# Attention and token/channel mixer on one core: two pools for the attention's tiles, three weight pairs decoded ahead, low parts on VectorE, tile addresses at multiples of 64 bytes

## The chip, the core and the metric

The kernel runs on one core of a Trainium2 chip. The metric is the time of one execution on the device in microseconds (us), lower is better. The core has a matmul engine (TensorE, PE in the profile), VectorE (DVE), ScalarE (ACT), GpSimd (POOL) and SyncE (SP), which issues all DMAs of this kernel. PEld is the loading of a matmul's weights, which the profile lists beside PE.

## What is computed

Causal attention with a decay, then a two-layer mixer over tokens and one over channels. The inputs are float32, and `B, H, S, D = 8, 8, 576, 64`; the model width is 512, the token mixer's inner width 256, the channel mixer's 1536.

```python
scores = (q @ k.T) / sqrt(D) + cum[:, None] - cum[None, :]   # cum = cumsum(log(clip(f)))
scores = where(causal, -1e9, scores)
attn = softmax(scores)
x = concat_heads(attn @ v)                         # (B, S, 512)
h = maximum(x.T @ w_tok1, 0) @ w_tok2              # over tokens
u = x + h.T
out = u + maximum(u @ w_ch1, 0) @ w_ch2            # over channels
```

The mixer's four weight matrices arrive as 64-bit floats in two 32-bit words each.

## The kernel before, in words

**Precision.** A float32 value is split into a high part that a fast matmul takes (fp32r) and a low part, the value minus the high part. A product is three matmuls: high x high, low x high, high x low. So nearly every tile comes in a pair: `hl`, `t1h`/`t1l`, `w1r[:, 0]`/`w1r[:, 1]`, and so on. ScalarE or GpSimd writes the high parts (`hi_act` L288, `hi_pool` L291); GpSimd's `lo_pool` (L294, `tensor_tensor` subtract) or VectorE's `lo_dve` (L297) and `lo_relu` (L300) write the low ones. The first four heads (`FQ`, `FV`) use plain fp32 matmuls and skip the split.

**Attention.** The 64 heads (`HB`) go one after the other, a pair of heads to a load. For each head: q and k are loaded and split, gathered by DMA (`k<-hl`, L533) into `k1` and `k2`; scores in five row blocks (L560), the causal mask and row minimum on VectorE (L567), the exponential on ScalarE (L574), the normalisation on GpSimd (L602), the transposes of the probabilities on PE (L616), their high and low parts, and the product with v (L684 to 698), folded into `xt`.

**Mixer.** After four heads of a batch follows half of its token mixer (`mixer`, L887: transposes L913, `tok1` L946, `tok2` L970), and after eight its other half and the first `F1 = 2` of the 12 blocks of the channel mixer (`ch1` L1015, `ch2` L1043); `u` and the partial sums are stored to DRAM. The other `F2 = 10` blocks run over all 4608 tokens at the end, in nine chunks of 512 columns (`up` L815 with matmuls L832 to 834, `down` L842 with L853 to 855). There each of the ten steps of a chunk takes 24 matmuls of 512 columns, 12 of `up` and 12 of `down`.

**Decoding weights.** Every block of the weights is turned from 64-bit words to fp32 and split by `decode` (L359): a load into `d_raw` (three buffers); s1 on ScalarE (L377); s2, s3, s4 on VectorE (L381, L385, L389); s5 (L393) on GpSimd for the 15 early blocks and on VectorE for the 20 late ones; s6 on VectorE (L397); the high part on ScalarE, the low part on GpSimd (L295). `d_g` (two buffers) holds the work between s1 and the low part. The 20 late decodes make the pairs `w1r[i]`, `w2r[i]` for i = 0 to 9, which the last stage needs in this order.

**Memory.** SBUF is full during the attention. The attention's tiles (`ATT`, L884) lie in one pool, `att`. When its last reader is done, `swap` (L1178) gives the whole pool back and lays `w1r`, `w2r` and `hid` there. In the plan this is an operation `gate` that follows every operation on an attention tile (L763 to 768), and the loads of the late decodes wait for it (`rd=["gate"] if late`, L368). Pools lay tiles in steps of 32 bytes: `ident` begins at byte 16,512 (258 x 64), and behind the small tiles `nmin`, `sums`, `rec` and `lower` (32 bytes) `t1h` begins at byte 19,872 (310 x 64 + 32). All tiles behind it have sizes that are multiples of 64 bytes, and so all of them begin at odd multiples of 32.

**What sets the order.** Nothing is scheduled on the chip. A planner (`Plan`, L82) simulates the five engines with costs for each operation (`mm_`, `tp_`, `d_act`, `d_dve`, `d_ptt`, L263 to 278) and starts, on each engine, the ready operation with the lowest priority number whose buffers are free. Priorities are the head's number plus an offset for the kind of operation (`OFF`, L23), plus one for the kind and the head in its batch (`STEP`, L29; `MIX`, L56, for the mixer). The simulated order is emitted as it is, each engine runs its own list in this order, and semaphores make it wait where data are not ready.

**Fills.** `fill` (L344) puts matmuls of `ident` with itself, of no use to the result, at the lowest priority: 60 of them, each two passes of 64 columns, not before 3.5 us of the plan and with 110 ns added after each.

Of the kernel before, what the change touches and what calls it, by code (L numbers as in the profile page):

```python
# [9 lines left out]
F32 = mybir.dt.float32  # L10
# [8 lines left out]
    FILL=60, EP=3, DB=0, DLAST=1, K0=0, F1=2, FQ=4, FV=4, LAG=4.11, n_raw=1, n_vr=2, n_hl=1, n_k1=2, n_k2=2, n_vv=2,  # L19
    E_hi='POOL', E_lo='POOL', E_vh='ACT', E_vl='POOL', E_nrm='POOL', n_pr=3, n_p34=2, n_p2=2, n_p1=1, n_p0=1, n_low=1,  # L20
    n_ring=12, n_part=4, n_xt=2, n_d_raw=3, n_d_g=2, n_hid=3, DEC3=7.97, SPREAD=10.82, SPREADA=5.72,
)
OFF = dict(  # L23
    load=-14.74, kh=45.74, kl=85.6, qh=-115.26, ql=-16.97, vh=-125.16, vl=123.08, s4=4.74, s3=5.74, s2=-18.62, mn=13.82,
    ex=6.93, rec=-24.46, nrm=-192.34, t3=3.49, t2=-86.91, t1=-83.66, t0=-30.56, hl=-22.74, av=6.05, fold=-23.02,
    fpe=3.13, lo0=-62.2, fev=-150.17, u=-45.03, dec=67.5, dec2=50.29, cd=-13.03, vload=-5.0,
# [3 lines left out]
    cd=(-18.28, 30.34, 0.0, -1.59, -7.08, 20.8, -4.45, -19.73),  # L30
    kh=(-13.25, -1.98, -14.84, -31.71, -0.08, 0.16, -4.73, -16.57),
    kl=(0.37, 23.35, 3.6, 16.35, -22.44, 19.22, -9.3, 14.29),
    s4=(-0.24, 11.93, 15.18, 0.0, 0.23, -18.99, 59.85, 19.27),
    s3=(-8.42, -2.23, -16.47, 3.1, -5.05, 3.69, -8.16, -5.03),
    s2=(-8.9, 5.94, 2.9, 7.66, -73.57, -5.62, -37.16, -17.06),
    mn=(-2.85, -2.59, -1.3, 27.24, -15.18, -23.44, 55.89, -2.52),
    ex=(8.73, 7.79, -3.58, -4.16, -24.69, 9.71, 15.25, -0.82),
    rec=(22.8, -0.87, 7.74, -8.31, -3.51, 14.08, 0.0, -15.0),
    nrm=(-0.65, -0.14, -0.26, -56.35, 0.93, 8.15, 15.62, 16.52),
    t3=(-0.21, -6.67, 3.6, -5.38, 7.93, -4.68, -63.6, 0.91),  # L40
    t2=(-8.37, 4.56, -28.86, -0.92, -2.2, 21.66, 9.34, -1.7),
    t1=(2.24, -60.09, 14.99, -0.13, 1.6, -10.19, -0.26, 18.37),
    t0=(-17.86, -45.26, -1.03, 6.15, -93.62, -1.53, 2.02, -1.16),
    hl=(-14.65, 3.9, 19.52, -2.31, 1.89, 47.46, 1.51, 21.22),
    av=(63.33, -8.47, -19.49, -11.27, -9.11, -24.95, -27.57, -16.6),
    fold=(0.0, -4.01, 0.0, 15.75, -6.44, -20.04, 54.83, -5.7),
    load=(0.44, -22.57, -32.0, 0.63, -21.63, 0.0, 24.57, -17.55),
    vload=(-3.66, -1.79, -4.01, 2.15, 1.75, -12.36, 4.68, -26.36),
    qh=(10.91, -1.93, 0.0, 6.38, 17.8, 15.93, -0.05, 13.38),
    lo0=(-19.38, -0.5, -4.34, -1.11, -3.76, 0.0, -12.38, 21.57),  # L50
    ql=(9.89, -8.85, -13.87, 15.7, 1.76, 0.12, 0.0, 25.12),
    vh=(-0.25, 1.03, -17.17, 0.0, -0.24, -3.2, 8.2, 72.18),
    vl=(6.57, -2.23, 2.05, 5.49, -2.18, -5.19, -2.35, -1.08),
# [3 lines left out]
    (-22.1, -17.41, -3.1, 2.93, 26.12, -0.37, 12.64, 5.86),  # L57
    (-10.33, 23.64, -53.62, -1.9, -30.51, 42.72, 7.26, -41.94, 25.22, -8.12, -7.09, 12.01, 3.03, 3.93, -39.21, -12.17, 8.18, 11.69, 19.72, 142.59, -29.87, -72.3, 9.6, -13.06, 8.97, 78.59, -11.05, 125.89),
# [19 lines left out]
class Op:  # L78
    __slots__ = ("eng", "dur", "head", "tail", "lat", "fn", "prio", "bufs", "need", "outs", "ready", "start", "idx")


class Plan:  # L82
# [43 lines left out]
    def run(self, slots):  # L126
# [18 lines left out]
        tail = dma_at = 0.0  # L145
# [30 lines left out]
        while left:  # L176
            moved = False
            for e, lst in ready.items():
# [23 lines left out]
                engine_at[e] = end  # L202
                heapq.heappush(events, (end, heap_id, None))
# [44 lines left out]
def build(nc, env, dims):  # L248
# [35 lines left out]
    def dma(prio, fn, nbytes, **k):  # L284
        return p.op("SP", k.pop("dur", 475), prio, fn, lat=nbytes / k.pop("rate", 360), **k)
# [24 lines left out]
    def decay():  # L310
# [12 lines left out]
        p.op("ACT", d_act(S, False), pr, lambda: nc.scalar.activation(row(0), row(0), AF.Ln), wr=["f"], bufs=[w])  # L323
        p.op(
# [3 lines left out]
        p.op("DVE", d_dve(S, True), pr, lambda: nc.vector.tensor_scalar(at(cc)[:, 0, :], c(), 1.0, None, op0=ALU.mult), rd=["c"], wr=["ch"], bufs=[cc])  # L328
        p.op("DVE", d_dve(S), pr, lambda: lo_dve(at(cc)[:, 1, :], c(), at(cc)[:, 0, :]), rd=["c", "ch"], wr=["cl"], bufs=[cc])
# [14 lines left out]
    def fill(i):  # L344
        av = Buf("av")
        p.op(
            "PE", [tp_(64, 64)] * 2, 1e6 + i, lambda: nc.tensor.matmul(at(av)[:64, :64], E["ident"][:, :64], E["ident"][:, :64], start=True, stop=True),
            rd=[("fill", i - 1)], wr=[("fill", i)], bufs=[av], lat=110, at=3500.0,
        )
# [9 lines left out]
    def decode(prio, loads, w, hi, lo, tok, late=False):  # L359
# [7 lines left out]
        for i, (rows, cols, src) in enumerate(loads):  # L367
            dma(prio - 1.0, lambda a=(rows, cols, src): ld(*a), nb / len(loads), rd=["gate"] if late else [], wr=[(rb, i)], bufs=[rb])  # L368
# [856 lines left out]
```

## Time and profile before

| | |
|---|---|
| median of three runs | 1129.55 us (1127.94 to 1131.58) |
| the profiled execution | 1131.37 us |
| its span, first to last instruction | 1129.6 us |
| TensorE clock granted, mean over the span | 0.979 |
| busy: PE, VectorE, ScalarE, GpSimd | 96%, 56%, 49%, 49% of the span |

A row of a group reads: line, engine, operation, output <- inputs with shapes, x count | busy us, mean ns of one | idle time of the engine just before these instructions, and what ended it. A row of a stage gives start:end, length, then for each engine its busy time with the number of instructions, the granted TensorE clock (1.00 is full), the share of time in which the DMA engines were busy, and GB/s. A wait reads: who <- whom, us in total, how often, the longest. In the timeline and in the chain of work that ended last, a row begins with its start and its length in us. Busy time of PE is modelled, since matmuls overlap: their pace is read from their starts or from a stretch without gaps.

### The profile page before, as it was taken

How to read it: one execution, taken by the hardware profiler on the slowest of the kernel's cores; microseconds unless marked ns; L12 is line 12 of the kernel's file. 1: busy time of each engine (PE TensorE's matmuls, PEld its weight loads, DVE VectorE, ACT ScalarE, POOL GpSimd, SP SyncE). 2: the span in 40 equal slices, each digit the busy share in tenths (PEclk: the TensorE clock that was granted, in tenths of full speed). 3: DMA queues.
4: the chain of work that ended last, by engine and by line, in shares of the span. 5: the costliest groups of instructions: out<-in, count | busy, mean ns of one | idle time of the engine just before them, and what ended most of it. 6: DMA issues, size and time to landing. Idle time of an engine off the chain costs nothing.

```text
span 1129.6 us, 18680 instructions
## 1 busy us (share of the span) xinstructions
PE 1084.4 (96%) x6422; PEld 940.4 (83%) x6422; DVE 637.1 (56%) x1598; ACT 554.8 (49%) x1440; POOL 552.4 (49%) x633
## 2 busy tenths in 40 slices
PE   8988899999999999999997889999999999999998
PEld 5667789999999998999996668888888888888886
DVE  5888887888778787787869993121212121211111
ACT  4677787888787887878854342111111111111110
POOL 4667797877787785977725335130303021211010
PEclk7998899999999999999998999999999999999999
DMA  8487767777777677777635444130303030302011
GB/s 203 111 197 166 191 148 205 204 170 193 207 190 211 173 197 182 189 202 191 156 120 177 139 133 140 46 112 1 113 1 112 1 112 1 112 2 73 20 56 38
DMA packets 70223, 146.65 MB, mean 130 GB/s; under 512 B 10048, under 2 KB 27456, under 8 KB 69104
## 3 DMA queue, kind: packets, MB, share of 16 engines
q1 hardware_dynamic: 70128, 145.45, 47.7%
q8 instruction: 51, 0.84, 0.3%
q14 instruction: 44, 0.36, 0.1%
HBM read 63.46 MB, written 28.31 MB: 81 GB/s over the span
## 4 chain that ended last, share of the span: by engine, by line
PE 66%; DVE 10%; DMA 9%; POOL 7%; issue 3%; ACT 2%; SPq 2%; DVEq 0%; POOLq 0%; ACTq 0%
DMA k<-hl 8%; PE pair L855 7%; PE bank L833 7%; PE pair L853 7%; PE pair L854 7%; PE bank L834 7%; PE bank L832 6%; PE bank L616 5%; PE bank L560 4%; DVE d_g L389 2%; PE pair L560 2%; POOL hl L489 2%; POOL pr L602 2%; PE pair L698 2%; PE pair L696 2%
## 5 line engine op out<-in xcount | busy, mean ns | idle before, releaser
L301 DVE SCALAR_TENSOR_TENSOR hid<-bank,hid 128x512 fp32r<-128x512 f32 x90 | 62.1, 690 | 331.9 <-ACT hid L289 331.9
L295 POOL TENSOR_TENSOR ring<-xt,ring 128x512 fp32r<-128x512 f32 (+1 forms) x68 | 92.6, 1378 | 273.2 <-ACT ring L289 272.7
L289 ACT ACTIVATE hid<-bank 128x512 fp32r<-128x512 f32 x90 | 53.7, 596 | 336.4 <-PE bank L834 336.4
L602 POOL TENSOR_SCALAR pr<-pr,rec 128x576 f32<-128x576 f32 (+4 forms) x320 | 167.4, 543 | 38.9 <-DVE rec L595 17.1
L832 PE MATMUL bank<-ring,w1r 128*128 128x512 f32 x360 | 141.2, 392 | 7.0 <-DVE hid L301 6.9
L289 ACT ACTIVATE p<-bank 128x384 fp32r<-128x384 f32 (+1 forms) x300 | 127.0, 474 | 30.1 <-PE bank L616 21.8
L616 PE MATMUL bank<-ident,pr 128*128 128x128 f32 (+1 forms) x960 | 137.7, 276 | 3.7 <-ACT pr L574 1.5
L833 PE MATMUL bank<-ring,w1r 128*128 128x512 f32 x360 | 140.8, 391 | 0.3 <-POOL w1r L295 0.3
L855 PE MATMUL pair<-hid,w2r 128*128 128x512 f32 x360 | 140.3, 390 | 0.7 <-DVE hid L301 0.7
L834 PE MATMUL bank<-ring,w1r 128*128 128x512 f32 x360 | 140.8, 391 | 0.0
L853 PE MATMUL pair<-hid,w2r 128*128 128x512 f32 x360 | 140.3, 390 | 0.0
L854 PE MATMUL pair<-hid,w2r 128*128 128x512 f32 x360 | 140.1, 389 | 0.0
L298 DVE TENSOR_TENSOR p<-bank,p 128x384 fp32r<-128x384 f32 x180 | 105.7, 594 | 39.1 <-ACT p L289 38.9
L574 ACT ACTIVATE pr<-bank,nmin 128x320 f32<-128x320 f32 (+3 forms) x256 | 117.9, 469 | 15.9 <-DVE nmin L567 10.3
L616 PEld LDWEIGHTS bank<-ident,pr 128*128 128x128 f32 (+1 forms) x960 | 107.7, 132 | 17.4 <-issue 4.3
L567 DVE CUSTOM_DVE_ANT_0 bank<-bank,mask 128x192 f32<-128x192 f32 (+3 forms) x256 | 106.5, 432 | 22.4 <-PE bank L560 20.8
L560 PE MATMUL bank<-k 128*128 128x320 f32 x480 | 86.2, 302 | 11.1 <-DMA k<-hl 8.4
L560 PEld LDWEIGHTS bank<-k 128*128 128x128 f32 x480 | 71.5, 178 | 22.6 <-issue 9.4
L832 PEld LDWEIGHTS bank<-ring,w1r 128*128 128x128 f32 x360 | 67.9, 189 | 23.4 <-DVE hid L301 9.6
L855 PEld LDWEIGHTS pair<-hid,w2r 128*128 128x128 f32 x360 | 67.5, 188 | 15.4 <-DVE hid L301 1.5
L833 PEld LDWEIGHTS bank<-ring,w1r 128*128 128x128 f32 x360 | 67.8, 188 | 14.6 <-POOL w1r L295 0.8
L834 PEld LDWEIGHTS bank<-ring,w1r 128*128 128x128 f32 x360 | 67.9, 189 | 14.3
(124 smaller groups left out, 2498.1 us busy)
## 6 DMA issues: line engine op xcount, KB each, us to landing
k<-hl SPq DMA_DIRECT2D x180, 288.0 KB
raw<-in_qk SPq DMA_DIRECT2D x30, 576.0 KB
vr<-in_v SPq DMA_DIRECT2D x32, 320.0 KB
ud<-xt SPq DMA_DIRECT2D x8, 1152.0 KB
pd<-part SPq DMA_DIRECT2D x32, 288.0 KB
out_t<-part SPq DMA_DIRECT2D x36, 256.0 KB
d_raw<-in_w_ch SPq DMA_DIRECT2D x12, 512.0 KB
d_raw<-in_w_ch SPq DMA_DIRECT2D x40, 128.0 KB
```

The costliest lines, as they stand in the source:

```text
L289: nc.scalar.activation(out, in_, func, scale=scale)
L560: nc.tensor.matmul(ps[:m, of : of + w], k[:, 0, i0 : i0 + m], k[:, 1, j0 : j0 + w], start=(x == 0), stop=(fq or x == 1))
L567: nc.vector.tensor_tensor_reduce(x, x, E["mask"][:m, a : a + w], -1.0 / D**0.5, 3e38, op0=ALU.add, op1=ALU.min, accum_out=E["nmin"][sm][:m ...
L574: nc.scalar.activation(at(pr)[:m, poff[t] : poff[t] + w], at(buf)[:m, of : of + w], AF.Exp, bias=E["nmin"][sm][:m, t : t + 1], scale=-1.0, ...
L602: nc.gpsimd.tensor_scalar(x, x, r, 0.0, op0=ALU.mult, op1=ALU.add)
L616: nc.tensor.transpose(out, at(pr)[:, poff[i] + start[j] : poff[i] + end[j]], E["ident"])
L832: nc.tensor.matmul(q, wh[:, c, :], h_, start=(c == 0), stop=False)
L833: nc.tensor.matmul(q, wl[:, c, :], h_, start=False, stop=False)
L834: nc.tensor.matmul(q, wh[:, c, :], l_, start=False, stop=(c == NC - 1))
L853: nc.tensor.matmul(q, wh, h_, start=(i == i0), stop=False)
L854: nc.tensor.matmul(q, wl, h_, start=False, stop=False)
L855: nc.tensor.matmul(q, wh, l_, start=False, stop=(i == NF - 1))
```

## The change

- The attention's tiles go into two pools. `raw`, `hl`, `k1`, `k2` and `cc`, which only the scores need, lie in one at the right end of SBUF, the others in one at the left. Each has its own gate. The first, after the last operation on a score tile, frees room for `w1r`, `w2r` of the first three pairs (`PAIRS0 = 3`) and `hid`; the second for the other seven.
- A late decode's load and steps s1 to s6 wait for no gate; the high part, the first that writes into the new pool, waits for its own.
- The low part of a late decode is `lo_dve` on VectorE, before `lo_pool` on GpSimd.
- The planner knows a port that GpSimd and the marked VectorE operations share: none of them starts in the plan while another holds it. It assumes slower DMAs (300 bytes per ns after 360, 220 after 200 for gathers), and the lag between scores and transposes is 3.3 heads after 4.11. All offsets are new, and the first and the last batch and each decode have offsets of their own.
- 120 fills, not before 8.5 us of the plan, without the added 110 ns.
- One exponential into `warm` after the logarithm of `f`. `warm` also takes 32 bytes behind `lower`, so that the tiles behind it begin at multiples of 64 bytes; `even0` and `even1` (32 bytes each) do the same for the pools at the right end.
- The two row blocks that share a bank are scored as 0, 3 and no longer as 3, 0.

```diff
-    FILL=60, EP=3, DB=0, DLAST=1, K0=0, F1=2, FQ=4, FV=4, LAG=4.11, ...
+    FILL=120, EP=3, DB=0, DLAST=1, F1=2, FQ=4, FV=4, LAG=3.3, ...
...
-    def op(self, eng, dur, prio, fn, rd=(), wr=(), bufs=(), lat=0, at=0.0):
+    def op(self, eng, dur, prio, fn, rd=(), wr=(), bufs=(), lat=0, at=0.0, port=False):
         o = Op()
+        o.port = port or eng == "POOL"
...
-                    if o.ready > t or (best is not None and (o.prio, o.idx) >= (best.prio, best.idx)):
+                    if o.ready > t or (o.port and port_at > t) or (best is not None and (o.prio, o.idx) >= (best.prio, best.idx)):
...
                 engine_at[e] = end
+                if o.port:
+                    port_at = end
...
+        p.op("ACT", 1400, pr, lambda: nc.scalar.activation(E["warm"], E["lower"], AF.Exp), rd=["f"], wr=["warm"])
...
-            rd=[("fill", i - 1)], wr=[("fill", i)], bufs=[av], lat=110, at=3500.0,
+            rd=[("fill", i - 1)], wr=[("fill", i)], bufs=[av], at=8500.0,
...
-            dma(prio - 1.0, lambda a=(rows, cols, src): ld(*a), nb / len(loads), rd=["gate"] if late else [], wr=[(rb, i)], bufs=[rb])
+            dma(prio - 1.0, lambda a=(rows, cols, src): ld(*a), nb / len(loads), wr=[(rb, i)], bufs=[rb])
...
-        p.op("ACT", d_act(w, False), prio, lambda: hi_act(hi(), asf(tl()[2])), rd=[gb], wr=[(tok, "h")], bufs=[gb])
-        p.op("POOL", d_ptt(w), prio, lambda: lo_pool(lo(), asf(tl()[2]), hi()), rd=[gb, (tok, "h")], wr=[(tok, "l")], bufs=[gb])
+        p.op("ACT", d_act(w, False), prio, lambda: hi_act(hi(), asf(tl()[2])), rd=[gb, *([late] if late else [])], wr=[(tok, "h")], bufs=[gb])
+        p.op(
+            "DVE" if late else "POOL", d_dve(w) if late else d_ptt(w), prio, lambda: (lo_dve if late else lo_pool)(lo(), asf(tl()[2]), hi()),
+            rd=[gb, (tok, "h")], wr=[(tok, "l")], bufs=[gb], port=True,
+        )
...
-                    late=True,
+                    late=f"gate{int(i >= PAIRS0)}",
...
-    gate = p.op("POOL", 1, HB + 2, lambda: E["swap"]())
...
+    for x, kinds in enumerate(ATT):
+        last = [q for q in p.ops if any(z.kind in kinds for z in q.bufs)]
+        gate = p.op("POOL", 1, HB + 2, lambda x=x: E["swap"](x))
...
+ATT = ("raw", "hl", "k1", "k2", "cc"), ("vr", "vv", "pr", "p34", "p2", "p1", "p0", "low")
+PAIRS0 = 3
...
+    E["warm"] = const.tile([P, 1], F32, name="warm")
...
+    att = [tc.tile_pool(name=f"att{x}", bufs=1, side=side) for x, side in enumerate(("right", "left"))]
...
+    ap[0].tile([P, 8], F32, name="even0")
...
+    def swap(x):
+        att[x].__exit__(None, None, None)
+        wp = ctx.enter_context(tc.tile_pool(name=f"wpool{x}", bufs=1, side=("right", "left")[x], reuse_waits="tile"))
+        for i in range(PAIRS0) if x == 0 else range(PAIRS0, F2):
+            for w in (1, 2):
+                E[f"w{w}r"].append(wp.tile([P, 2, C], F32R, name=f"w{w}r{i}"))
+        if x == 0:
+            tiles(wp, "hid", [P, 2, 512], F32R, PRM["n_hid"])
+            wp.tile([P, 8], F32, name="even1")
```

More of the change, by code (lines that the diff above doesn't have):

```diff
@@ L284, in dma @@
     def dma(prio, fn, nbytes, **k):
-        return p.op("SP", k.pop("dur", 475), prio, fn, lat=nbytes / k.pop("rate", 360), **k)
+        return p.op("SP", k.pop("dur", 475), prio, fn, lat=nbytes / k.pop("rate", 300), **k)
     def hi_act(out, in_, scale=1.0, func=AF.Copy):
@@ L352, in build, with decode @@
         fill(i)
-    def decode(prio, loads, w, hi, lo, tok, late=False):
+    def decode(prio, loads, w, hi, lo, tok, late=None):
         rb, gb = Buf("d_raw"), Buf("d_g")
@@ L467, in build @@
     for i, fn in enumerate(first):
-        fn(-50 + i if i < PRM["K0"] else 1 + 5.5 * i / len(first) + o_dec)
+        fn(1 + 5.5 * i / len(first) + o_dec + DEC[i])
     for i, fn in enumerate(second):
-        fn(7 + 5.0 * i / len(second) + o_dec + OFF["dec2"])
+        fn(7 + 5.0 * i / len(second) + o_dec + OFF["dec2"] + DEC[len(first) + i])
     xts = {}
@@ L495, in build @@
         b, h = divmod(n, H)
-        o = {k: OFF[k] + x[h] for k, x in STEP.items()}
+        o = {k: OFF[k] + x[h] + (EARLY[k][h] if b == 0 else 0.0) + (LATE[k][h] if b == B - 1 else 0.0) for k, x in STEP.items()}
         fq, fv = n < FQ, n < FV
@@ L762, in build @@
     base = HB + 20
-    last_heads = [q for q in p.ops if any(z.kind in ATT for z in q.bufs)]
-    gate = p.op("POOL", 1, HB + 2, lambda: E["swap"]())
-    for q in last_heads:
-        q.outs.append(gate)
-        gate.need += 1
-    p.writer["gate"] = [gate]
+    for x, kinds in enumerate(ATT):
+        last = [q for q in p.ops if any(z.kind in kinds for z in q.bufs)]
+        gate = p.op("POOL", 1, HB + 2, lambda x=x: E["swap"](x))
+        for q in last:
+            q.outs.append(gate)
+            gate.need += 1
+        p.writer[f"gate{x}"] = [gate]
     for i, fn in enumerate(third):
-        fn(HB + 2 + PRM["DEC3"] * i)
+        fn(HB + 2 + PRM["DEC3"] * i + (OFF["dec3"] if i < 2 * PAIRS0 else 0.0))
     def pieces(a, z):
@@ L1064, in mixer @@
     for i, (c, f) in enumerate(us):
[L1065 removed]
+        f(n + 1 + PRM["LAG"] + o["fpe"] + MIX[part][i] + (MIXE[part][i] if b == 0 else 0.0) + (MIXL[part][i] if b == B - 1 else 0.0) + (PRM["SPREAD"] if part else PRM["SPREADA"]) * done / total)
         done += c
@@ L1177, in attn_mixer_kernel @@
         E[kind] = {(("part", i),): E["part"][(("part", i),)]}
-    def swap():
-        att.__exit__(None, None, None)
-        wp = ctx.enter_context(tc.tile_pool(name="wpool", bufs=1))
-        for w in (1, 2):
-            E[f"w{w}r"] = [wp.tile([P, 2, C], F32R, name=f"w{w}r{i}") for i in range(F2)]
-        tiles(wp, "hid", [P, 2, 512], F32R, PRM["n_hid"])
+    E["w1r"], E["w2r"] = [], []
+    def swap(x):
[7 more added lines that the diff above has]
+            wp.tile([P, 8], F32, name="even1")
     E["swap"] = swap
```

162 lines of the change are left out of this document (110 added, 52 removed).

## The prediction

> **What bounds the kernel now.** I read the page first, then the busy time of each engine by stage, then the groups, waits and timeline of the stages that stood out.
>
> ```profile
> span 1129.6 us, 18680 instructions
> PE 1084.4 (96%) x6422; PEld 940.4 (83%) x6422; DVE 637.1 (56%) x1598; ACT 554.8 (49%) x1440; POOL 552.4 (49%) x633
> ```
>
> Busy time by stage; after the bounds and the length come PE, PEld, DVE, ACT and POOL, then the granted TensorE clock, the DMA share and GB/s:
>
> ```profile
> 15.00:32.00 17.00, 16.34 (x55) 10.12 (x56) 8.69 (x31) 8.49 (x26) 5.91 (x10) 0.50 0.69 181
> 32.00:112.00 80.00, 73.15 (x437) 53.51 (x435) 69.14 (x198) 58.29 (x169) 57.52 (x77) 0.96 0.66 158
> 112.00:560.00 448.00, 435.36 (x3299) 410.86 (x3298) 364.19 (x1072) 359.62 (x1013) 346.92 (x421) 0.99 0.74 188
> 560.00:590.00 30.00, 30.00 (x237) 29.34 (x236) 17.83 (x40) 17.88 (x45) 9.19 (x15) 1.00 0.33 119
> 590.00:680.00 90.00, 74.24 (x354) 61.76 (x352) 87.08 (x118) 38.89 (x70) 35.95 (x27) 0.92 0.48 154
> 680.00:760.00 80.00, 79.65 (x357) 66.00 (x356) 17.82 (x26) 15.02 (x27) 29.69 (x24) 1.00 0.30 93
> 760.00:1100.00 340.00, 340.00 (x1502) 281.53 (x1501) 58.98 (x87) 49.79 (x85) 58.68 (x46) 1.00 0.16 52
> ```
>
> PE's 96% is a mean over stages with different limits. From 680 us on PE alone is the bound: no gap, full clock, VectorE mostly idle; only cheaper matmuls can shorten it. In the attention (112 to 560) PE is idle for 448 - 435.4 = 12.6 us, and VectorE, ScalarE and GpSimd are each about 80% busy: PE first, the order of the work second. Two stages have another limit. In 590:680, where attention turns into the channel MLP, VectorE is busy for 87.1 of 90 us and PE idle for 15.8 at a clock of 0.92. At 15:32 PE is busy at half its clock.
>
> **The transition: early pairs, and the low part on VectorE.** The groups of VectorE, then those of GpSimd, in 590:680 (busy us, mean ns | idle before):
>
> ```profile
> L389 DVE SCALAR_TENSOR_TENSOR d_g<-d_raw,d_g 128x512 f32<-128x512 uint32 x19 | 25.5, 1341 | 0.5
> L393 DVE TENSOR_TENSOR d_g<-d_g 128x512 f32<-128x512 f32 x19 | 18.1, 951 | 0.6
> L397 DVE SCALAR_TENSOR_TENSOR d_g<-d_raw,d_g 128x512 uint32<-128x512 uint32 x19 | 14.0, 736 | 0.4
> L385 DVE TENSOR_SCALAR d_g<-d_g 128x512 uint32<-128x512 uint32 x20 | 13.4, 670 | 0.5
> L381 DVE TENSOR_SCALAR d_g<-d_g 128x512 uint32<-128x512 uint32 x20 | 9.2, 460 | 0.2
> ```
>
> ```profile
> L295 POOL TENSOR_TENSOR w1r<-d_g,w1r 128x512 fp32r<-128x512 f32 x10 | 13.4, 1337 | 29.4 <-ACT w1r L289 29.4
> L295 POOL TENSOR_TENSOR ring<-xt,ring 128x576 fp32r<-128x576 f32 (+1 forms) x8 | 12.4, 1560 | 10.3 <-ACT ring L289 10.3
> L295 POOL TENSOR_TENSOR w2r<-d_g,w2r 128x512 fp32r<-128x512 f32 x9 | 11.8, 1308 | 23.2 <-ACT w2r L289 23.2
> ```
>
> The 20 late decodes are the stage: 80.2 of the 87.1 us, 4.16 us each (the five means added). Single instructions of the timeline show what they cost undisturbed, and what disturbs them:
>
> ```profile
> 606.17 0.69 DVE L397 SCALAR_TENSOR_TENSOR d_g<-d_raw,d_g 128x512 uint32<-128x512 uint32 x1
> 606.78 0.42 DVE L381 TENSOR_SCALAR d_g<-d_g 128x512 uint32<-128x512 uint32 x1
> 607.24 0.43 DVE L385 TENSOR_SCALAR d_g<-d_g 128x512 uint32<-128x512 uint32 x1
> 607.70 1.74 DVE L389 SCALAR_TENSOR_TENSOR d_g<-d_raw,d_g 128x512 f32<-128x512 uint32 x1
> ...
> 618.52 0.69 DVE L393 TENSOR_TENSOR d_g<-d_g 128x512 f32<-128x512 f32 x1
> ```
>
> ```profile
> 607.61 1.28 POOL L295 TENSOR_TENSOR w1r<-d_g,w1r 128x512 fp32r<-128x512 f32 x1 [2.02 <-ACT w1r L289]
> 585.05 4.97 SPq L365 DMA_DIRECT2D d_raw<-in_w_ch  x9
> ```
>
> An instruction with two SBUF inputs takes 0.69 us, one with a single input 0.43; the 1.74 us L389 lies beside a GpSimd low part that began 0.1 us earlier, and ends about 0.5 us after it. Undisturbed, a decode is 3 x 0.69 + 0.43 + 0.42 = 2.92 us. The stage's 19 decodes' worth of two-input and 20 of single-input instructions would then be 57 x 0.69 + 20 x 0.85 = 56.3 us; 80.2 - 56.3 = 23.9 us is blocking, 0.89 us for each of GpSimd's 10 + 8 + 9 = 27 instructions.
>
> The change takes 19 of those 27 from GpSimd (the low parts), and gives VectorE one more two-input instruction for each decode, which I take at the same 0.69. New VectorE time: 20 x (2.92 + 0.69) = 72.2, plus 8 x 0.89 = 7.1 of blocking by what GpSimd keeps, 79.3 us; before, 20 x 4.16 = 83.2. Alone that is 3.9 us saved. The larger part is the start. Before, the plan holds even the loads behind the one gate (SP issues the first at 585); now loads and the first six steps wait for buffers alone, and three of ten pairs go into the pool that is free after the last score matmul. In 560:590 VectorE is idle for 30 - 17.8 = 12.2 us, three decodes' worth. Together 16.1 us, against a ceiling of 15.8 us of idle PE and 0.08 x 90 = 7.2 of lost clock. I take 14, because that idle time lies in pieces; bounds 0 and 23. Next late is PE itself. What VectorE's longer queue holds up:
>
> ```profile
> PE bank L832 <- DVE hid L301: 6.9, 5, 1.8
> ACT d_g L377 <- POOL w1r L295: 10.1, 8, 1.7
> ```
>
> Behind a decode stands the low part of `hid` (L301), and PE waits for it (first row of the waits in that stage): one more 0.69 in front of each of ten would be 6.9 us, which belongs to the slow rival below. The second row's wait, ScalarE for a `d_g` buffer that GpSimd still reads, gets a nearer releaser. The 20 loads' transfers cost nothing: DMA share 0.33 in 560:590. Two pools issue no instruction of their own.
>
> **The start: fills and the exp table.** The first three rows are of the timeline, the last two of the chain that ended last:
>
> ```profile
> 7.67 4.88 PE L347 MATMUL pair<-ident 128*64 128x64 f32 x78
> 15.66 0.87 PE L560 MATMUL bank<-xt 66*128 66x320 f32 x1 [3.10 <-DMA xt<-cc]
> 18.86 1.28 ACT L574 ACT_TABLE_LOAD   x1 [2.31 <-DVE nmin L567]
> ```
>
> ```profile
> 15.66 3.95 PE bank L560 x8
> 33.76 1.88 PE bank L560 x8
> ```
>
> Sixty more fills are 120 more matmuls at 4.88/78 = 0.063 us, 7.5 us of PE. About 3.1 us of it covers the wait ahead of the first score; the rest lies in gaps, or, at worst, costs 4.4 us. What it can buy is clock: the same eight score matmuls take 3.95 us at half clock and 1.88 later, and the whole of 15:32 would be 8.2 us shorter at full clock. But in that row PE was busy for 16.3 of 17 us and the clock stayed at 0.50, so scores alone do not lift it here. I take the first eight only, 2.1 us. The Trainium skill (TensorE: Matmul & The Clock Gate, "What's actually happening") would have the full clock return after about 3.4 us of sustained work; by that rule the whole 8.2 us would be within reach, and the trace disagrees, since 16 us of work did not bring it back. The warm-up exponential takes the 1.28 us table load off the first softmax, where ScalarE is ahead anyway; I take 0.9. Start: -3, bounds +4.4 and -9.5.
>
> **The rewritten order.** All other offsets are new, and the planner now bars GpSimd and the marked VectorE steps from overlapping. No row prices an order. PE's idle time in 32:560 is 6.9 + 12.6 = 19.5 us, which is the ceiling. On the other side, if 112:560 became as gappy as 32:112 (8.6% instead of 2.8%), it would cost 26 us. I take -4, nearer to the smooth stage as that is most of the work. The shorter lag (3.3 heads after 4.11) and the slower assumed DMA rates are part of this.
>
> **Aligned operands.** Before, `lower` leaves every tile behind it at an odd multiple of 32 bytes; `ident` lies at a multiple of 64. No run shows a full-pace matmul at 64. Rows from the chain, then from PE's timeline:
>
> ```profile
> 40.98 0.97 PE pair L560 x4
> 241.08 1.31 PE bank L616 x12
> ```
>
> ```profile
> 597.31 0.29 PE L972 MATMUL bank<-t2h,ring 128*128 128x288 f32 x1
> ...
> 598.10 0.29 PE L972 MATMUL bank<-t2h,ring 128*128 128x288 f32 x1
> ```
>
> The fp32 scores (288 columns, 242.5 ns each) and the transposes (128 columns, 109.2) run at (242.5 - 109.2)/160 = 0.833 ns a column plus 2.5 ns, although the scores' operands are at odd multiples of 32: no penalty at half pace. At full pace six matmuls of 288 take 0.79 us, 131.7 each, and 512 columns take 340/1502 = 226.4; at 0.417 ns a column that leaves 11.7 and 13.1 ns. So there is a fixed 10.6 ns that half pace does not pay, and the address may be its cause or not. Bounds 0 and -10.6 ns a matmul; above nothing I see no way, since no tile gets a worse address. I take 0, by the nearest row, the same matmul on the old addresses. The Trainium skill (same page, "Wait — 56ns, not 53.3ns?") gives about 2.5 ns above the columns for any warm matmul, which is what half pace shows and full pace does not; were its figure reached, the result would be the first rival's.
>
> **Sum.** -14 - 3 - 4 = -21 us. The profiled execution took 1131.4 us (span 1129.6 and 1.8 around it), so 1110.4; it lies 1.8 above the median 1129.55, so against the median 1108.5. Its own range, 1096 to 1122.
>
> **Rivals.** *Aligned matmuls are faster.* From 680 us the 357 + 1502 and some 110 last matmuls save 10.6 ns each, 21 us, with nothing beside them to absorb it. In the attention roughly 2,300 of 3,299 matmuls run at full pace and save some 8 ns, 18 us, of which I allow half, as the other engines are at 80%. For it: the surplus at full pace is real and unexplained. Against: misaligned half-pace operands pay nothing. 1108.5 - 30 = 1078.
>
> *VectorE gets blocked more, slower than before.* The early decodes now run beside attention work on GpSimd, whose instructions are longer:
>
> ```profile
> L489 POOL TENSOR_TENSOR hl<-raw,hl 128x1152 fp32r<-128x1152 f32 x27 | 72.1, 2670 | 1.7
> ```
>
> With x us of blocking a decode, the decodes end where they did when 72.2 + 20x = 83.2 + 12.2, at x = 1.16; the forecast has 0.36, before it was 23.9/19.5 = 1.2. At x = 1.8, four two-input instructions meeting one or two such neighbours, they end 12.8 us later, and fills outside gaps take away the start's gain: 1129.5 + 12.8 - 3 = 1139.
>
> *It does not start early.* If the first pool's last reader ends near 585, VectorE gains the 3.9 us of blocking and little else, the order washes out and fills eat the start: 1126.
>
> **Numbers.** A measurement of this kernel tells about 0.3%, 3.4 us. Forecast 0.50, faster matmuls 0.25, blocked VectorE 0.14, no early start 0.11. Faster: 0.50 + 0.25 and a little of the last, 0.77; same 0.09; slower 0.14. The range, 1072 to 1130, takes in the first rival and the unchanged time, and leaves out the slow one and the fringe below.
>
> **What would show it.** Right: decode instructions on VectorE before 590; L389 and L393 near 0.7 to 0.9 us; PE idle for under 5 us between the last attention matmul and 680; first full-rate MLP stretch some 15 us earlier, then the same 226 ns a matmul. Half clock should still appear after the first scores. Wrong: 216 ns a matmul in the MLP (first rival); late decodes of 4.5 us and more, or low parts that stand in front of `hid` (second); first late decode after 585 (third); more than 20 us of idle PE in 112:560 would break the order's term.

## The result and the profile after

After takes 1136.5 us (median of 20 runs, 1130.5 to 1145.7), before 1130.9 us in the same session (20 runs, 1125.2 to 1135.3). The ratio is 1.0059, with a 95% interval of 1.0042 to 1.0076: slower by 0.6%. The forecast was 1108.5, in a range of 1072 to 1130. The profiled execution of after took 1141.6 us (span 1139.8), 10.2 more than that of before.

The page of after, its length and its engines:

```profile
span 1139.8 us, 18916 instructions
...
PE 1091.6 (96%) x6542; PEld 949.7 (83%) x6542; DVE 624.7 (55%) x1618; ACT 559.3 (49%) x1441; POOL 524.9 (46%) x613
```

Busy time by stage of after; the columns are those of the same view of before:

```profile
15.00:32.00 17.00, 17.00 (x75) 11.49 (x75) 7.03 (x30) 7.39 (x24) 7.30 (x14) 0.53 0.62 155
...
112.00:560.00 448.00, 415.99 (x3126) 391.08 (x3125) 344.80 (x1005) 335.94 (x934) 327.46 (x397) 0.98 0.72 183
560.00:590.00 30.00, 30.00 (x232) 29.15 (x232) 23.53 (x72) 22.76 (x63) 20.83 (x26) 1.00 0.74 193
590.00:680.00 90.00, 88.11 (x549) 79.15 (x548) 84.08 (x158) 53.68 (x114) 23.65 (x24) 1.00 0.42 134
...
760.00:1100.00 340.00, 340.00 (x1501) 281.53 (x1500) 59.01 (x87) 49.40 (x85) 62.59 (x49) 1.00 0.18 56
```

Two things stand here at once. The stage 590:680 did what was forecast: PE is busy for 88.1 of 90 us instead of 74.2, at full clock instead of 0.92. And PE's idle time in 112:560 rose from 12.6 to 448 - 416.0 = 32.0 us, past the 20 that the prediction had named as the end of its term for the order. The MLP is untouched: 340/1501 = 226.5 ns a matmul.

A stage with fixed borders mixes two effects here, since the attention now ends at another time. A cut at the work itself is cleaner. All instructions of one source line, with the times of the first and the last (the p.v products of the attention, then the up products of the MLP); before, then after:

```profile
L698 PE MATMUL pair<-p,vv x240: 218/332/628, 73.2 to 586.6; 128*128 128x512 f32 x60, 128*128 128x128 f32 x60
L832 PE MATMUL bank<-ring,w1r x360: 389/389/628, 620.4 to 1118.7; 128*128 128x512 f32 x180
```

```profile
L769 PE MATMUL pair<-p,vv x240: 220/331/628, 70.5 to 618.4; 128*128 128x512 f32 x60, 128*128 128x128 f32 x60
L904 PE MATMUL bank<-ring,w1r x360: 389/389/397, 642.6 to 1128.6; 128*128 128x512 f32 x180
```

Line 769 of after is line 698 of before, and 904 is 832; the replayed kernels below have them at 705 and 843, or near. The last attention matmul moved from 586.6 to 618.4 us, a loss of 31.8. From it to the last up matmul it is 1118.7 - 586.6 = 532.1 us before and 1128.6 - 618.4 = 510.2 after, a gain of 21.9. These two lengths, "the attention's end" and "the rest", are given for every run below. 31.8 - 21.9 = 9.9, nearly the whole 10.2 us between the two profiles; the medians of all runs are 5.6 apart.

### The profile page after: what moved, and what is told of

Same layout as the page of the kernel before. It is cut to its first block, busy times and chain, and to the rows that moved or that the text cites. A ratio compares the mean times of both kernels' runs of the same rounds, so it can differ in the third digit from the quotient of the medians.

```text
span 1139.8 us, 18916 instructions
## 1 busy us (share of the span) xinstructions
PE 1091.6 (96%) x6542; PEld 949.7 (83%) x6542; DVE 624.7 (55%) x1618; ACT 559.3 (49%) x1441; POOL 524.9 (46%) x613
## 4 chain that ended last, share of the span: by engine, by line
PE 72%; DMA 11%; DVE 6%; POOL 4%; ACT 3%; SPq 3%; issue 2%; DVEq 0%; POOLq 0%; ACTq 0%
DMA k<-hl 9%; PE bank L905 7%; PE bank L906 7%; PE bank L904 7%; PE pair L927 7%; PE pair L926 7%; PE pair L925 7%; PE bank L687 5%; PE bank L631 5%; PE pair L631 2%; POOL hl L560 2%; PE pair L769 2%; PE pair L767 2%; SPq L604 1%; ACT pr L645 1%
## 5 line engine op out<-in xcount | busy, mean ns | idle before, releaser
L355 ACT ACTIVATE hid<-bank 128x512 fp32r<-128x512 f32 x90 | 53.9, 599 | 344.5 <-PE bank L906 344.4
L355 ACT ACTIVATE p<-bank 128x384 fp32r<-128x384 f32 (+1 forms) x300 | 130.4, 474 | 39.8 <-PE bank L687 35.2
L687 PE MATMUL bank<-ident,pr 128*128 128x128 f32 (+1 forms) x960 | 140.9, 278 | 8.0 <-POOL pr L673 4.7
L645 ACT ACTIVATE pr<-bank,nmin 128x448 f32<-128x448 f32 (+3 forms) x256 | 118.2, 468 | 38.7 <-DVE nmin L638 33.5
L638 DVE CUSTOM_DVE_ANT_0 bank<-bank,mask 64x64 f32<-64x64 f32 (+3 forms) x256 | 106.5, 431 | 35.9 <-PE bank L631 28.7
L631 PE MATMUL bank<-k 128*128 128x320 f32 (+1 forms) x480 | 88.3, 310 | 13.0 <-DMA k<-hl 11.0
L631 PEld LDWEIGHTS bank<-k 128*128 128x128 f32 (+1 forms) x480 | 65.4, 180 | 19.0 <-DMA k<-hl 7.6
L926 PEld LDWEIGHTS pair<-hid,w2r 128*128 128x128 f32 x360 | 67.6, 188 | 14.1
L906 PEld LDWEIGHTS bank<-ring,w1r 128*128 128x128 f32 x360 | 67.6, 188 | 14.1
L904 PEld LDWEIGHTS bank<-ring,w1r 128*128 128x128 f32 x360 | 67.6, 188 | 14.0
L925 PEld LDWEIGHTS pair<-hid,w2r 128*128 128x128 f32 x360 | 67.5, 188 | 14.0
```

What stands on the lines that cost most here:

```text
L355: nc.scalar.activation(out, in_, func, scale=scale)
L631: nc.tensor.matmul(ps[:m, of : of + w], k[:, 0, i0 : i0 + m], k[:, 1, j0 : j0 + w], start=(x == 0), stop=(fq or x == 1))
L645: nc.scalar.activation(at(pr)[:m, poff[t] : poff[t] + w], at(buf)[:m, of : of + w], AF.Exp, bias=E["nmin"][sm][:m, t : t + 1], scale=-1.0, ...
L687: nc.tensor.transpose(out, at(pr)[:, poff[i] + start[j] : poff[i] + end[j]], E["ident"])
L904: nc.tensor.matmul(q, wh[:, c, :], h_, start=(c == 0), stop=False)
L906: nc.tensor.matmul(q, wh[:, c, :], l_, start=False, stop=(c == NC - 1))
```

## The experiments

**The theories.** A: the rewritten order of the attention, which the prediction priced at -4 us, costs 20 to 30, whatever the addresses, fills and decodes do; the transition gains as forecast. B: the new addresses slow the attention. C: what the late decodes do ahead of the gate slows it (blocked VectorE, SP's queue, decode buffers). D: the low parts on VectorE are all that the transition gains by.

An order can't be kept by keeping the planner's numbers, because the planner lays everything out anew when one duration changes. So most kernels here replay an order: the planner is run once as it was, and then again with the change, while each engine may only take its next instruction of the first run. The late decodes and the gates are free:

```diff
+                    if keep and not o.late and keep[e][-1] != o.idx:
+                        continue
                     if o.ready > t or (best is not None and (o.prio, o.idx) >= (best.prio, best.idx)):
                         continue
```

All results in one table; the ratio is to before on the same chip, the last two columns are of the profiled execution, in us:

| run | ratio to before, 95% interval | attention's end | the rest |
|---|---|---|---|
| before | 1 | 586.6 | 532.1 |
| after | 1.0059 (1.0042 to 1.0076) | 618.4 | 510.2 |
| aligned_alone | 1.0003 (0.9984 to 1.0022) | 583.5 | 531.9 |
| odd_after | 1.0058 (1.0028 to 1.0088) | 616.5 | 510.2 |
| graft | 0.9981 (0.9957 to 1.0006) | 592.7 | 520.7 |
| graft_low_gpsimd | 1.0110 (1.0086 to 1.0134) | 595.1 | 532.9 |
| reverse_graft | 1.0269 (1.0235 to 1.0303) | 606.6 | 540.1 |
| after_60_fills | 1.0088 (1.0054 to 1.0122) | 614.3 | 510.1 |
| graft_gated | 0.9895 (0.9863 to 0.9927) | 587.7 | 517.9 |
| graft_slack | 1.0003 (0.9979 to 1.0028) | 581.8 | 527.0 |
| after_gated | 1.0076 (1.0051 to 1.0101) | 610.0 | 514.5 |
| graft_after_w2 | 0.9978 (0.9953 to 1.0002) | 592.4 | 522.0 |
| gated_slack | 0.9891 (0.9861 to 0.9921) | 584.1 | 518.4 |
| swap_replanned | 1.0456 (1.0418 to 1.0495) | 630.6 | 537.9 |
| order_alone | 1.0164 (1.0125 to 1.0202) | 615.2 | 520.2 |
| before_then_after | 1.0059 (1.0036 to 1.0082) | 606.2 | 520.0 |
| after_then_before | 1.0107 (1.0060 to 1.0154) | 618.4 | 518.8 |

**The addresses, one way and the other.** In before a tile of 4 bytes a partition is added behind `lower`, which shifts all that follow by 32 bytes; in after `warm` is widened and the two spacers go, which shifts all by 32 again. Every engine's order stays.

```diff
+    E["warm"] = const.tile([P, 1], F32, name="warm")      # before, aligned
```

```diff
-    E["warm"] = const.tile([P, 1], F32, name="warm")
+    E["warm"] = const.tile([P, 9], F32, name="warm")[:, :1]      # after, at odd multiples of 32
-    ap[0].tile([P, 8], F32, name="even0")
-            wp.tile([P, 8], F32, name="even1")
```

> Before, with every TensorE operand tile moved by 32 bytes to a multiple of 64 and nothing else: the same instructions in the same order. Theory A (the rewritten order alone costs the change its gain, addresses are indifferent): the time of before, 1128 to 1134 us, 226.4 ns a matmul in the MLP. Rival B (the new addresses slow the attention): up to the 31 us that the attention lost, about 1160. The prediction's first rival (aligned matmuls are faster): about 1100, 216 ns a matmul.

> After, with every TensorE operand tile put back at an odd multiple of 32 bytes: the order of every engine is that of after. Theory A: the time of after, 1133 to 1140 us. Rival B (the new addresses slow the attention): the lost 31 us come back, about 1106.

Neither shift moved the time, and both profiles show 340 us for 1502 matmuls in 760:1100, as before. Theory B falls, and so does the prediction's first rival: the address of a TensorE operand, at 32 or 64 bytes, costs nothing here in either direction.

**The change without its order.** Before's order is replayed; the two pools, the early loads and steps and the low parts on VectorE are put in, then the same with the low parts left on GpSimd. The late decodes have the lowest priority here: they take the time that the replayed order leaves.

```diff
-    order = p.run(slots_of())
+    order = p.run(slots_of(), keep)      # before's order; pools, early decodes, low parts and addresses of after
```

> Before's order written out and replayed for every instruction but the late decodes, with the two pools, the early pairs, the low parts on VectorE and the aligned tiles of after; no more fills, no warm-up exponential. Theory A: attention as in before (last attention matmul near 587 us, idle PE in 112:560 near 13 us), transition as in after (21 us gained), so 1110 us, 1104 to 1118. Rival C (pools, early decodes or low parts slow the attention themselves): idle PE in 112:560 of 25 us and more, 1125 to 1140.

> The graft with the late low parts left on GpSimd: splits the transition's gain. The prediction gave the low parts 3.9 us and the early start 12: theory A by these terms 1114 us, 1110 to 1120. Rival D (the low parts are the whole gain, the early start nothing): 1126 to 1132.

The graft's two rows, then those with the low parts on GpSimd:

```profile
L705 PE MATMUL pair<-p,vv x240: 220/331/522, 73.8 to 592.7; 128*128 128x512 f32 x60, 128*128 128x128 f32 x60
L843 PE MATMUL bank<-ring,w1r x360: 389/389/397, 627.4 to 1113.4; 128*128 128x512 f32 x180
```

```profile
L705 PE MATMUL pair<-p,vv x240: 220/331/522, 71.3 to 595.1; 128*128 128x512 f32 x60, 128*128 128x128 f32 x60
L843 PE MATMUL bank<-ring,w1r x360: 389/389/632, 633.5 to 1128.0; 128*128 128x512 f32 x180
```

The graft was expected at 1110 and came at 1125.6. Both of its parts missed: the rest gained 11.4 us instead of 21, and the attention ended 6 us later than before's. So theory A is not all: something in the structure costs the attention a few us, which is theory C in small. In the second kernel the early start alone gains nothing (532.9 against 532.1); with the low parts on VectorE the rest is 12.2 us shorter. That is theory D, as far as before's order goes, though at 1140.6 us the kernel is slower than either theory had it, since its attention also ends 8.5 us after before's.

**The order without the change, and the fills.** After's order is replayed with the late decodes as before had them; and after without the fills 61 to 120.

```diff
+ rd=[late] if late and old else []      # loads of late decodes behind one gate, which waits for all of the attention
+ "DVE" if late and not old else "POOL"  # low parts on GpSimd
```

```diff
-lambda: nc.tensor.matmul(
+lambda: i >= 60 or nc.tensor.matmul(
```

> After's own order replayed for every instruction but the late decodes, and these put back as before: no load, step or write of a late decode ahead of the last attention instruction, low parts on GpSimd. Theory A (the order of the attention costs about 30 us, whatever the decodes do): the last attention matmul stays at 610 us or later, and with the transition's gain gone the time is 1150 to 1170 us. Rival C (early decodes and low parts slow the attention): the last attention matmul comes back to 590 us or earlier, and the time to 1135 or less.

> After with fills 61 to 120 left out (their 120 matmuls of 64 columns have no effect on the output), everything else in the same order. If the added fills lie in PE's idle time, as the prediction's sum has it: 1133 to 1140 us, no change. Rival: they stand in front of attention matmuls and cost up to their own 7.5 us: 1129. If they held up the clock: more half clock, and up to 1145.

```profile
L776 PE MATMUL pair<-p,vv x240: 221/319/628, 70.7 to 606.6; 128*128 128x512 f32 x60, 128*128 128x128 f32 x60
L914 PE MATMUL bank<-ring,w1r x360: 388/389/632, 631.6 to 1146.7; 128*128 128x512 f32 x180
```

1158.6 us is in the expected span, but the attention's end at 606.6 lies between the two theories: after's order alone is 20 us later than before's, and some 12 us come on top in after. The second 60 fills do nothing that shows: the intervals of 1.0088 and 1.0059 overlap, and without them PE is idle for 53.7 us of the span instead of 48.2.

**The early steps held back.** In the graft, all late loads wait for the last score matmul, so that no late decode touches the attention. A second kernel also leaves the order after 540 us of the plan free, plans the late steps on VectorE 1.3 times as long, and gives each late decode a priority by its place instead of the lowest.

```diff
-rd=["gate0"] if late and not new["early"] else [], wr=[(rb, i)], bufs=[rb]
+rd=["gate0"] if late else [], wr=[(rb, i)], bufs=[rb]
```

> The graft, with every late load held until the last score matmul is done, so that no step of a late decode lies in the first 565 us. The graft lost 6 us of idle PE in the attention against before. If the five or so early steps and loads did that (theory A with a price for early steps): last attention matmul at 584 to 588 us, total 1117 to 1122. Rival (the addresses or the pools did it): last attention matmul at 592 again, 1125.

> The gated graft, with the order after 540 us of the plan left free and the late VectorE steps planned 1.3 times as long, so that mixer evictions no longer stand behind decodes. In the graft PE waited 9.5 us between the last attention matmul and the first up matmul, mostly for VectorE's ring writes. If the order of VectorE's queue is what costs there: that wait under 4 us and the total 1108 to 1115. Rival (VectorE's amount of work is the limit, not its order): no better than the gated graft.

The gated graft's attention ends at 587.7, as expected. At 1115.7 us, a little under the expected span, it is 1.05% faster than before and the first kernel that beats both. What the early steps did in the graft can be seen in one place. VectorE, GpSimd and PE of the graft there (start, duration, and for PE the idle time ahead with what ended it):

```profile
146.99 4.38 DVE L387 TENSOR_SCALAR d_g<-d_g 128x512 uint32<-128x512 uint32 x1 [0.48 <-ACT d_g L383]
151.29 0.44 DVE L307 SCALAR_TENSOR_TENSOR ring<-bank,ring 128x288 fp32r<-128x288 f32 x1
```

```profile
146.21 2.62 POOL L496 TENSOR_TENSOR hl<-raw,hl 128x1152 fp32r<-128x1152 f32 x1
148.82 2.73 POOL L609 TENSOR_SCALAR pr<-pr,rec 128x576 f32<-128x576 f32 x5
```

```profile
151.79 0.96 PE L567 MATMUL bank<-k 128*128 128x448 f32 x4 [4.47 <-DVE ring L307]
```

The first VectorE step of an early decode, 0.42 us undisturbed (L381 in before), takes 4.38 while GpSimd works through six instructions; the mixer's ring write stands behind it, and PE is idle for 4.5 us. That is about the size of the loss in this graft: of the 5.0 us between the two attention ends, 2.1 are there at the first p.v product already (73.8 against 71.7), ahead of any late load. The second kernel kept the attention (581.8) but not the rest (527.0): the last decodes came later (last high part at 674.9 after 662.3), and PE waited for them inside the MLP (24.5 us busy in 650:680, where the gated graft has 30.0). As its rival had it, that is no better than the gated graft.

**Where the early steps cost, and more slack.**

```diff
+ rd=["gate0"] if late and held else []          # after_gated: after's own order, late loads behind the last score matmul
+ rd=[(("w2", F1 - 1), "l")] if late else []     # graft_after_w2: late loads behind the last early decode
+ dur = dur * 1.15                               # gated_slack: late VectorE steps in the plan of the gated graft
```

> After, its own order replayed, with every late load held until the last score matmul is done. In after the last attention matmul ran at 618 us, in the reverse graft at 607. If the early steps of the late decodes cost after about 11 us (theory A with a price for early steps): last attention matmul at 604 to 609 us, and a total of 1124 to 1130. Rival (what the reverse graft regained came from elsewhere, the low parts or the gate): 616 again, total 1136.

> The graft, with the late loads held only until the last of the early decodes (the mixer's second weight) is written, about 160 us; two late decodes and a third load still lie in the attention. In the graft the first matmul that uses that weight came at 177 us, in the gated graft at 167. If the late decodes cost the attention by taking the decode buffers ahead of the early ones: last attention matmul at 584 to 589 us, total 1114 to 1119, as gated. Rival (the steps and loads themselves cost, wherever they lie): 592 us and 1125.

> The gated graft, with the late VectorE steps planned 1.15 times as long, all else replayed: fewer of them stand ahead of mixer evictions. If VectorE's queue order costs the 7.7 us that PE still waits ahead of the first up matmul: 1109 to 1113. Rival (what is gained there comes back as waits for decodes in the MLP): 1115 to 1118 as the gated graft, or more.

After with its late loads held: its p.v products and its stage 15:32.

```profile
L775 PE MATMUL pair<-p,vv x240: 221/332/415, 62.4 to 610.0; 128*128 128x512 f32 x60, 128*128 128x128 f32 x60
15.00:32.00 17.00, 17.00 (x108) 11.63 (x107) 13.00 (x54) 11.13 (x40) 8.61 (x15) 1.00 0.82 191
```

The attention ends at 610.0, 8 us earlier than in after, and 4 us are given back in the rest. In the time nothing is left of that: 1136.8, a miss. The 8 us are not shown to be a price of the early steps: this profile ran its 15:32 at full clock, its first p.v product starts at 62.4 instead of 70.5, and from the first to the last it takes 547.6 us where after takes 547.9. So the 12 us of the reverse graft stay open between the early steps, the low parts and the later gate. The expectation that the decode buffers were the trouble fell too: with the late loads behind the last early decode the attention ends at 592.4, as in the graft. In before's order, then, early loads and steps cost in both places that were tried. The last kernel repeats the gated graft's time (1115.9) without a gain.

**What an order is worth.** One edit in before that adds and removes nothing, with the planner left free to make its order anew.

```diff
-        for ts, kind in (((4,), "s4"), ((3, 0), "s3"), ((2, 1), "s2")):
+        for ts, kind in (((4,), "s4"), ((0, 3), "s3"), ((2, 1), "s2")):
```

> Before with one edit: in one of the three score groups the two tiles are taken in the other order, as after does, and the planner makes its order anew with before's numbers. The edit adds and removes nothing. If the numbers fit only the plan that they were chosen for (theory A: an order is worth tens of us, and any edit asks for a new one): 1150 to 1170 us. Rival (the planner's rules carry the order, the numbers only trim it): 1125 to 1135.

```profile
112.00:560.00 448.00, 412.25 (x2992) 381.59 (x2993) 335.95 (x974) 329.13 (x916) 315.92 (x384) 0.97 0.67 174
```

1179.3 us, 4.6% slower, beyond what was expected: 35.8 us of idle PE in 112:560 where before has 12.6, with the same instructions. So before's numbers fit the plan for which they were chosen and did not carry over this edit. What the swap costs within before's own order was not run; it is also a part of the change.

**The order alone, and in two halves.** The gated graft in everything, with after's order in place of before's, whole and for one part of the plan each. Two details of after are not in the replay: the two row blocks are scored as 3, 0, and the 60 fills stand in the places of after's second 60, so that none runs at the start.

```diff
-    keep = ...      # before's order
+    keep = ...      # after's order; or one of the two for what its plan starts before 300 us, the other for the rest
```

> The gated graft in everything (pools, gate, low parts, addresses, 60 fills), except that all instructions but the late decodes stand in after's order instead of before's. This is the order's price with nothing else changed. Theory A (the order costs 20 us and more in the attention): last attention matmul at 604 to 612 us against 587.7, total 1125 to 1140 against 1115.7. Rival (the loss came from fills, lag of the warm-up or the early steps, not from the order): 584 to 592 us, 1112 to 1120.

> The gated graft with before's order for what its plan starts in the first 300 us, and after's order for the rest. If after's order loses its time while the mixer's first weights are decoded and its first batches run (112:224 had 10 of the 19 us of added idle PE): last attention matmul at 588 to 594 us. If it loses evenly: 596 to 602.

> The mirror: after's order for what its plan starts in the first 300 us, then before's. If the loss is early: last attention matmul at 600 to 610 us. If it is spread evenly: 596 to 602.

The gated graft, then the same kernel in after's order: busy PE of the page, source rows (the third is that of the fills), the stage row, and two waits in 112:560 (us, times, longest).

```profile
PE 1076.7 (96%) x6422; PEld 935.2 (84%) x6422; DVE 629.6 (56%) x1618; ACT 555.8 (50%) x1440; POOL 529.0 (47%) x613
L705 PE MATMUL pair<-p,vv x240: 220/332/628, 71.7 to 587.7; 128*128 128x512 f32 x60, 128*128 128x128 f32 x60
L843 PE MATMUL bank<-ring,w1r x360: 389/389/397, 619.7 to 1105.6; 128*128 128x512 f32 x180
L353 PE MATMUL pair<-ident x120: 222/222/370, 1.9 to 76.6; 128*64 128x64 f32 x120
```

```profile
112.00:560.00 448.00, 432.83 (x3278) 407.41 (x3277) 362.18 (x1061) 357.09 (x1001) 347.16 (x419) 1.00 0.73 186
```

```profile
POOL hl L488 <- DMA k<-hl: 1.0, 2, 0.7
ACT pr L581 <- DVE nmin L574: 4.8, 14, 0.8
```

```profile
PE 1091.5 (95%) x6422; PEld 947.6 (83%) x6422; DVE 624.0 (54%) x1618; ACT 558.1 (49%) x1440; POOL 522.3 (46%) x613
L705 PE MATMUL pair<-p,vv x240: 220/331/628, 68.1 to 615.2; 128*128 128x512 f32 x60, 128*128 128x128 f32 x60
L843 PE MATMUL bank<-ring,w1r x360: 389/389/398, 649.5 to 1135.4; 128*128 128x512 f32 x180
L353 PE MATMUL pair<-ident x120: 222/222/369, 73.3 to 181.7; 128*64 128x64 f32 x120
```

```profile
112.00:560.00 448.00, 421.59 (x3172) 394.19 (x3171) 341.16 (x1013) 338.58 (x950) 327.49 (x399) 0.98 0.71 181
```

```profile
POOL hl L488 <- DMA k<-hl: 25.0, 9, 6.4
ACT pr L581 <- DVE nmin L574: 30.2, 30, 3.4
```

The instructions are the same and their order differs. The attention ends 27.5 us later (587.7 to 615.2), and the time goes from 0.9895 to 1.0164 of before, about 30 us and more than was expected. The fills' places are not after's, so this pair alone doesn't price after's order. But after's order with all its 120 fills loses too: 20.0 us in the reverse graft against before, and 22.3 in after_gated against the gated graft, though its first p.v product came 9.3 us earlier. So the order is worth 20 to 27.5 us at the attention's end, and theory A holds for its main part.

About half of the price in this pair is not waiting. PE's idle time over the span goes from 1116.5 - 1076.7 = 39.8 to 1146.3 - 1091.5 = 54.8 us; the other 14.8 us are the same 6,422 matmuls at a lower granted clock, 0.975 after 0.989 (over the six runs of each, 0.969 to 0.979 after 0.986 to 0.990). Whether the added gaps bring the clock down wasn't tested.

The halves don't place the loss: with after's order only behind 300 us the attention ends 18.5 us later, with it only ahead of 300 us 30.7 us later (that profile too has no fills at the start, ran its 32:112 at a clock of 0.81 where the others have 0.94 to 0.98, and is 7 us longer than the median of its runs). Both parts lose and the two don't add up to the whole, so the seam seems to have a price of its own: with after's order behind 300 us PE is idle for 13.1 us in 336:448, in the whole order for 6.2. Neither expectation was met.

What stays open is which of after's offsets does it. Of the engines' waits in 112:560 the two shown grow most, by 24 and 25 us: GpSimd's for `hl`, and that of ScalarE's exponential for the row minima. GpSimd can't write the next head pair until SP's gathers have read the last, and these need key buffers that PE frees. Whether one of these waits paces the attention or only follows a late PE wasn't tried; a second `hl` would take 9,216 bytes a partition while SBUF is full.

## Why the prediction was wrong

**What bounds the kernel** was read rightly: the MLP did not move, and the gain lay in the transition.

**The transition, -14 (0 to -23): inside its bounds, with the wrong split.** Its groups on VectorE in 590:680 of after:

```profile
L461 DVE TENSOR_TENSOR d_g<-d_g 128x512 f32<-128x512 f32 x15 | 11.7, 782 | 0.1
L465 DVE SCALAR_TENSOR_TENSOR d_g<-d_raw,d_g 128x512 uint32<-128x512 uint32 x14 | 10.8, 768 | 0.0
L457 DVE SCALAR_TENSOR_TENSOR d_g<-d_raw,d_g 128x512 f32<-128x512 uint32 x15 | 10.3, 687 | 0.2
L449 DVE TENSOR_SCALAR d_g<-d_g 128x512 uint32<-128x512 uint32 x15 | 8.6, 572 | 0.0
L453 DVE TENSOR_SCALAR d_g<-d_g 128x512 uint32<-128x512 uint32 x15 | 6.8, 453 | 0.1
L364 DVE TENSOR_TENSOR w2r<-d_g,w2r 128x512 fp32r<-128x512 f32 x8 | 6.7, 838 | 0.0
L364 DVE TENSOR_TENSOR w1r<-d_g,w1r 128x512 fp32r<-128x512 f32 x8 | 5.6, 697 | 0.0
```

The five means are 3.26 us, and the low part adds (6.7 + 5.6)/16 = 0.77: 4.03 us a decode, where the prediction's 79.3 us for 20 give 3.97. PE's waits in that stage are what was hoped for, and `hid` no longer appears among them:

```profile
PE bank L1045 <- DVE ring L367: 1.4, 1, 1.4
PE pair L757 <- DVE xt L817: 0.2, 1, 0.2
```

The gated graft, which has before's order, gains 532.1 - 517.9 = 14.2 us in the rest, the very 14, which is luck given the split; after gains 21.9, close to the bound. With its late loads held after gains 17.6, so some 4 us belong to the decodes ahead; what the rest beyond 14 comes from isn't shown. Wrong was the split. The prediction gave the low parts 3.9 us and the early start 12.2; by the two grafts the low parts are worth 12.2 and the early start without them nothing. The trace of after shows why. Step s5 of the late decodes (L461; the early decodes run it on GpSimd) in 170:590, then in 680:760, and ScalarE between the two (high parts L355, step s1 of the next decodes L445):

```profile
L461 DVE TENSOR_TENSOR d_g<-d_g 128x512 f32<-128x512 f32 x2 | 1.5, 750 | 0.0
```

```profile
L461 DVE TENSOR_TENSOR d_g<-d_g 128x512 f32<-128x512 f32 x4 | 2.8, 689 | 0.1
```

```profile
599.38 0.64 ACT L355 ACTIVATE w1r<-d_g 128x512 fp32r<-128x512 f32 x1
600.66 0.65 ACT L355 ACTIVATE w2r<-d_g 128x512 fp32r<-128x512 f32 x1
603.96 0.68 ACT L445 ACTIVATE d_g<-d_raw 128x512 f32<-128x512 f32 x1
```

Only two of the twenty come early, at 231 and 249 us, and none in 560:590, where the prediction had put three. More than two can't run ahead of the gate: the steps don't wait for it, but `d_g` has two buffers, and a decode gives its own back only after its low part, which follows the gated high part. In after's order the last score matmul runs at 595.8 us (565.2 in before), the first two high parts follow at 599.4 and 600.7, and only then, at 604.0, does the third decode begin. The attention's own work, which ran later, also kept VectorE at 23.5 us in 560:590. Three or four s5 come behind 680, beside the MLP, where they hold up nothing.

**The start, -3 (+4.4 to -9.5): no gain in the time is shown.** The first scores of after, then its table load:

```profile
13.54 3.82 PE L631 MATMUL bank<-xt 66*128 66x320 f32 x8 [1.68 <-DMA xt<-cc]
```

```profile
5.71 1.28 ACT L391 ACT_TABLE_LOAD   x1
```

The eight score matmuls take 3.82 us, still half pace, and 15:32 runs at a clock of 0.53; the -2.1 for them was wrong, and the remark beside it, that 16 us of PE work had not lifted the clock, was the better guide. The load is out of the softmax, the scores start 2.1 us earlier and the first p.v product 2.7 us (70.5 after 73.2). Of the added fills nothing reaches the end, since after without them takes the same time; the exponential wasn't taken out by itself. The half clock isn't fixed here: in the profile of after_gated, which has the same start, 15:32 ran at 1.00 and the first p.v product came another 8.1 us earlier, about the prediction's 8.2 for the whole stretch. In the time of its 12 runs this doesn't show.

**Early steps of late decodes, priced at nothing in the attention: wrong, by 3 to 5 us of the attention's end in before's order.** The graft against the gated graft: 592.7 to 587.7 (2.1 of it at the first p.v product already), and 0.9981 to 0.9895 in the time. In after's order no such price is shown. The second rival had this mechanism, a decode blocked by the attention's longer GpSimd instructions, but looked for it in how late the decodes end; it struck at what stood behind the blocked step on VectorE.

**The rewritten order, -4 (+26 to -19.5): the step that failed.** It measures 20 to 27.5 us at the attention's end, by the reverse graft, after_gated and the order alone. The upper bound has the size, partly by luck: it counted idle PE time alone, and in the pair that differs by the order half of the price is a lower granted clock. With it in place of the chosen value the prediction's own sum is -14 - 3 + 26 = +9 us, and the profiles differ by +10; that is luck too, since the transition gave more than 14 and the attention lost 31.8. The failure is the choice between the ends: the smooth stage 112:560 was taken as what any order gives there, and it was a property of before's order. (Of the assumed DMA rates only that of the loads is slower; the gathers' 220 after 200 bytes per ns is faster.) The swap of two tiles, replanned, shows how little holds it: 4.6%, some 51 us, for an edit of no cost. And no rival had the order as its mechanism, so the chance of slower went to another one.

**Aligned operands, 0: right**, in both directions. The 10.6 ns that a matmul pays at full pace and not at half pace are still without a cause.

**Chances.** The sign was wrong. A stage that bounds half of the span, an order of it with every number changed, and a bound of +26 made a case of its own, which would have had to be priced at about the forecast plus 30 and kept inside the range.

## What to carry to other kernels

Where instructions run in a fixed order on each engine, the order is a cost like an instruction, here worth 20 to 50 us of 1130: when a diff rewrites it, carry both of its ends through the sum and make it a rival. Compare two profiles by cutting at the last instruction of a stage, not at fixed times: it showed at once a gain of 22 and a loss of 32. Work that is moved ahead into a busy stage can be paid for by what is queued behind it; in before's order, holding it back to the stage's end gave the version that beats both kernels (0.9895, 0.9863 to 0.9927). Before counting on an early start, follow its buffers to the step that gives them back.

## What the runs showed of the hardware

A VectorE step of 0.42 us with one SBUF input took 4.38 us beside GpSimd, from a low part of 2.62 us through five short normalizations of 2.73 in all, and ended about with the last of them (151.37 and 151.55 us; spans of GpSimd are rough). The Trainium skill (SBUF — State Buffer, "SBUF: two separate sides") has the shared pair as an exclusive lock that whoever starts first keeps for the whole instruction. The trace agrees with the first 1.8 us, to the end of the low part; that VectorE did not get its turn between the five instructions behind it goes further than the rule as stated.

Much of the spread between runs of one kernel goes with TensorE's granted clock. The 12 runs of graft_slack go from 1121.4 us at a mean of 0.986 to 1136.5 at 0.977, and those of before from 1123.2 at 0.988 to 1138.2 at 0.978. A straight line through the runs gives 10.2 us for 0.01 of clock in graft_slack and 11.6 in the 20 runs of after (correlations -0.91 and -0.87); the 29 runs of before beside aligned_alone show less of it (4.1 us, -0.36). So a difference of a few us between two single profiles says little by itself.
